# Padding the weight and activation tiles of a two-layer FFN by 32 bytes each

## The chip, the cores and the metric

The kernel runs on one core of one Trainium2 chip. The metric is the device time of one execution in microseconds (us), lower is better; a time of a kernel is the median over several runs, and the profile is of one execution.

## The reference

Talking-heads attention, then a gated feed-forward layer, then a second one; all in float32. B = 2, 12 heads, 448 positions, head size 64, so that 896 tokens of 768 features go through the two layers.

```
scores = (q @ k.T) / 8;  scores = mix(scores, w_pre)      # over heads
attn = softmax(scores);  attn = mix(attn, w_post)
x = (attn @ v) as [896, 768]
g = x @ w_gate;  u = silu(g) * (x @ w_val)                # d_ff 1536
x2 = u @ w_out
h = x2 @ w_in;   g = h * clip(h + 3, 0, 6) / 6            # d_ff 2048
out = g @ w_out2
```

## The kernel before

Attention comes first, some 205 us of the profiled span, and nothing in it is touched. Then five stages follow one another, named in the trace by the tiles that they fill: g and v in turn (12 output chunks each; PSUM tiles `pg`, `pv`), o (6 chunks, `po`), i (16 chunks, `pi`) and p (6 chunks, `pp`). A chunk is 128 output features for all 896 tokens, in two halves (`hf`) of 448 tokens.

Accuracy needs more than one product. Every operand is split into a high part (rounded to the type float32r) and a low part (the rest), and `product_half` makes three matmuls for each 128 input features: high weights by high activations, high weights by low activations, low weights by high activations, all 128x128 by 448 columns. There are 2448 of them: 36 for a g, v or i chunk, 72 for an o chunk, 96 for a p chunk.

The loop over `subs` (a sub is a chunk, or a part of one where the input has more than 768 features) keeps the weights ahead of the products. For sub j it issues, in this order: `halve(j+1)`, the split of the next weights (high part a copy on ACT, low part a subtraction on DVE, L402 and L404); `finish` of the sub before (PSUM to activations, on ACT and DVE); `convert(j+2)`, which makes float32 out of the 64-bit words that are loaded (ACT, then four DVE instructions, L462); the split of the activations just made (`rest()`: high part on ACT, L652; low part on POOL, L653); `fetch(j+3)`, the load of raw weights from SP's queue (L451); and the matmuls. All of DVE's work stands in one queue in this order.

The tiles are allocated from both ends of a partition's memory. From the left: `act`, the sixteen activation tiles a0 to a15, that hold u (12 of them) and later g (16), each 7168 bytes: high and low part by two halves of 448 float32r. From the right: raw and converted weights of the first two subs (`early`), four tiles `big` (x and x2, high and low, 10752 bytes each), the split weights of subs 0 and 1 (`wp0`), and `wp`: two raw tiles (`wr`), two converted (`wy`), three high and three low tiles of split weights (`wh`, `wl`, 3072 bytes each) and four scratch tiles (`sg`, 1792 bytes each).

In the program's allocation table this gives these start addresses in a partition, modulo 512: activation tiles all 160; x and x2 all 416; `wr`, `wy`, `wh`, `wl` all 96; `sg` 96 and 352 in turn. Inside a tile the slices are 1792 bytes (activations: 3.5 times 512) or 512 bytes (weights) apart. So, whatever tile a matmul uses, its activations start 64 bytes after its weights modulo 256 (64 or 320 modulo 512).

Of the kernel before, what the change touches and what calls it, by code (L numbers as in the profile page):

```python
# [8 lines left out]
F32R = mybir.dt.float32r  # L9
# [7 lines left out]
B, H, S, D = 2, 12, 448, 64  # L17
# [31 lines left out]
def kernel(  # L49
# [34 lines left out]
    pools = {"early": ctx.enter_context(tc.tile_pool(name="early", bufs=1, side="right"))}  # L84
# [311 lines left out]
        return y, todo  # L396

    def split_w(pool, y, kc, name):
        hi = pool.tile([128, kc, 128], F32R, name=f"h{name}", tag="wh", bufs=2 if pool is pools["wp0"] else 3)
        lo = pool.tile([128, kc, 128], F32R, name=f"l{name}", tag="wl", bufs=2 if pool is pools["wp0"] else 3)  # L400
        hi_flat, lo_flat = (x.rearrange("p k f -> p (k f)") for x in (hi, lo))
        nc.scalar.copy(hi_flat, y)  # L402
        eng = nc.gpsimd if pool is pools["wp0"] else nc.vector
        eng.tensor_tensor(lo_flat, y, hi_flat.bitcast(F32), ALU.subtract)  # L404
        return hi, lo
# [13 lines left out]
                pass  # L419

    def new_pair(nm, tg):
        t = act.tile([128, 2, 2, S], F32R, name=nm, tag=tg)
        return [(t[:, 0, hf, :], t[:, 1, hf, :]) for hf in range(2)]

    steps = []
# [38 lines left out]
    def halve(j):  # L464
        if j < len(subs):
            kind, idx, k0, kc, _ = subs[j]
            _, y, _ = ys.pop(j)
            pool = pools["wp0" if j < 2 else "wp"]
            whl[j] = split_w(pool, y, kc, f"{kind}{idx}_{k0}")
# [169 lines left out]
    act = ctx.enter_context(tc.tile_pool(name="act", bufs=1, side="left"))  # L639
# [7 lines left out]
    def finish(kind, idx, pp):  # L647
# [7 lines left out]
        if kind == "g":  # L655
            for hf in range(2):
                sg = scratch(f"sg{idx}_{hf}")
                nc.scalar.activation(sg, pp[hf][:, :S], AF.Sigmoid)
                nc.vector.tensor_tensor(sg, pp[hf][:, :S], sg, ALU.mult)
                sgs[hf] = sg  # L660
        elif kind == "v":
            us.append(new_pair(f"u{idx}", f"a{idx}"))
            for hf in range(2):
                sg = sgs[hf]
                nc.vector.tensor_tensor(sg, pp[hf][:, :S], sg, ALU.mult)
                late.append((us[-1][hf], sg, nc.gpsimd))
        elif kind == "o":
            for hf in range(2):
                if hf not in x2:
                    x2[hf] = [big.tile([128, HP, S], F32R, name=f"x2{part}{hf}", tag="big") for part in "hl"]  # L670
                parts(of_x2(idx, hf), pp[hf][:, :S], nc.vector)
        elif kind == "i":
            gs.append(new_pair(f"g{idx}", f"a{idx}"))
            for hf in range(2):
                sg = scratch(f"rl{idx}_{hf}")
                nc.scalar.activation(sg, pp[hf][:, :S], AF.Relu, bias=half, scale=1.0 / 6.0)
                nc.vector.scalar_tensor_tensor(sg, sg, 1.0, pp[hf][:, :S], ALU.min, ALU.mult)  # L677
                late.append((gs[-1][hf], sg, nc.gpsimd))
        else:
            for hf in range(2):  # L680
                o, sz = HALVES[hf]
                ob = scratch(f"ob{idx}_{hf}")
                nc.scalar.copy(ob, pp[hf][:, :S])
                nc.sync.dma_start(out=outT[idx * 128 : (idx + 1) * 128, o : o + sz], in_=ob)
# [104 lines left out]
```

## Time and profile before

| | us |
|---|---|
| median of three runs | 687.66 |
| the runs | 687.36, 687.66, 691.33 |
| the profiled execution's own time | 685.68 |
| its span, first to last instruction | 683.9 |

The profiled execution is 1.98 us under the median, and 1.78 us of it lie outside the span. Of the span PE is busy 98%, DVE 74%, ACT 43% and POOL 22%; the granted TensorE clock is 1.00 throughout. A busy time of PE includes the pipelined ends of matmuls, so that two matmuls in a row overlap in it: how fast they go is read from the distance of their starts.

### The profile page before, as it was taken

How to read it: one execution, taken by the hardware profiler on the slowest of the kernel's cores; microseconds unless marked ns; L12 is line 12 of the kernel's file. 1: busy time of each engine (PE TensorE's matmuls, PEld its weight loads, DVE VectorE, ACT ScalarE, POOL GpSimd, SP SyncE). 2: the span in 40 equal slices, each digit the busy share in tenths (PEclk: the TensorE clock that was granted, in tenths of full speed). 3: DMA queues.
4: the chain of work that ended last, by engine and by line, in shares of the span. 5: the costliest groups of instructions: out<-in, count | busy, mean ns of one | idle time of the engine just before them, and what ended most of it. 6: DMA issues, size and time to landing. Idle time of an engine off the chain costs nothing.

```text
span 683.9 us, 16079 instructions
## 1 busy us (share of the span) xinstructions
PE 667.5 (98%) x6685; PEld 566.0 (83%) x6685; DVE 505.5 (74%) x836; ACT 297.1 (43%) x603; POOL 147.2 (22%) x179
## 2 busy tenths in 40 slices
PE   9989999999899999999999999999999999999997
PEld 3456656566689999999999999999999999999997
DVE  4678789898548888888887566668888888665550
ACT  4557667676433434343433323234554453332320
POOL 2423435435301131113111000013334332000000
PEclk9999999999999999999999999999999999999999
DMA  6767774554212423342333323322332233454420
GB/s 223 216 203 204 209 204 137 170 154 139 94 46 96 135 96 118 113 138 95 110 121 116 115 93 107 124 93 93 108 123 93 92 92 118 150 157 145 150 66 27
DMA packets 34200, 86.86 MB, mean 127 GB/s; under 512 B 9328, under 2 KB 22016, under 8 KB 34128
## 3 DMA queue, kind: packets, MB, share of 16 engines
q1 hardware_dynamic: 26208, 81.14, 36.6%
q0 software_dynamic: 7200, 3.94, 2.5%
q8 instruction: 52, 0.85, 0.5%
q10 hardware_dynamic: 720, 0.76, 0.3%
q14 instruction: 20, 0.16, 0.1%
HBM read 62.37 MB, written 2.75 MB: 95 GB/s over the span
## 4 chain that ended last, share of the span: by engine, by line
PE 67%; DVE 21%; DMA 5%; ACT 4%; issue 1%; SPq 1%; ACTq 0%; DVEq 0%
PE pp L413 15%; PE po L413 13%; PE pv L413 12%; PE pg L413 12%; DVE yi L462 9%; DMA sx<-S 5%; PE pqk L170 3%; PE pav L293 3%; PE ppre L217 3%; PE ppost L263 3%; DVE rl L677 2%; PE p L413 2%; DVE yp L462 2%; DVE li L404 2%; ACT e L238 2%; DVE nm L230 2%
## 5 line engine op out<-in xcount | busy, mean ns | idle before, releaser
L413 PE MATMUL pp<-g,hp 128*128 128x448 f32 x384 | 107.5, 361 | 0.0
L413 PE MATMUL po<-u,ho 128*128 128x448 f32 x288 | 80.6, 361 | 0.0
L653 POOL TENSOR_TENSOR g<-rl,g 128x448 fp32r<-128x448 f32 x32 | 41.3, 1310 | 167.8 <-ACT g L652 167.8
L413 PEld LDWEIGHTS pp<-g,hp 128*128 128x128 f32 x384 | 71.9, 187 | 5.5
L238 ACT ACTIVATE e<-ppre,nm 128x448 f32<-128x448 f32 x90 | 56.2, 630 | 38.9 <-DVE nm L230 38.7
L206 POOL DMA_DIRECT2D sx<-S x90 | 52.0, 578 | 93.9 <-issue 21.2
L413 PE MATMUL pp<-g,lp 128*128 128x448 f32 x192 | 69.8, 364 | 0.2 <-DVE lp L404 0.2
L413 PE MATMUL pi<-x2h,li 128*128 128x448 f32 x192 | 69.7, 363 | 0.0
L413 PE MATMUL pi<-x2l,hi 128*128 128x448 f32 x192 | 69.6, 362 | 0.0
L413 PE MATMUL pi<-x2h,hi 128*128 128x448 f32 x192 | 69.1, 360 | 0.0
L653 POOL TENSOR_TENSOR u<-sg,u 128x448 fp32r<-128x448 f32 x24 | 32.6, 1379 | 151.7 <-ACT u L652 151.7
L263 PE MATMUL ppost<-wn,e 60*64 60x60 f32 x2520 | 53.5, 221 | 4.1 <-issue 3.4
L413 PEld LDWEIGHTS po<-u,ho 128*128 128x128 f32 x288 | 54.0, 187 | 3.9
L230 DVE TENSOR_REDUCE nm<-ppre 128x1 f32<-128x448 f32 x90 | 52.0, 616 | 4.9 <-PE ppre L217 3.0
L217 PE MATMUL ppre<-sx,W 64*64 64x448 f32 x360 | 52.4, 545 | 2.0 <-issue 1.2
L293 PEld LDWEIGHTS pav<-at,v 128*64 128x64 f32 x576 | 28.0, 136 | 31.7 <-ACT xs L336 15.3
L263 PEld LDWEIGHTS ppost<-wn,e 60*64 60x64 f32 x2520 | 46.4, 134 | 7.9 <-issue 3.8
L413 PE MATMUL po<-u,lo 128*128 128x448 f32 x144 | 52.3, 363 | 0.0
L170 PE MATMUL pqk<-k,q 64*64 64x448 f32 (+3 forms) x384 | 48.5, 547 | 1.0 <-issue 1.0
L413 PE MATMUL pg<-xh,lg 128*128 128x448 f32 x132 | 47.9, 363 | 0.0
L413 PE MATMUL pv<-xh,lv 128*128 128x448 f32 x132 | 47.9, 363 | 0.0
L413 PE MATMUL pg<-xl,hg 128*128 128x448 f32 x132 | 47.8, 362 | 0.0
(97 smaller groups left out, 1397.2 us busy)
## 6 DMA issues: line engine op xcount, KB each, us to landing
sx<-S SPq DMA_DIRECT2D x90, 182.0 KB
ri<-in_moe_w_in_dram SPq DMA_DIRECT2D x16, 768.0 KB
ro<-in_moe_w_out_dram SPq DMA_DIRECT2D x12, 768.0 KB
rg<-in_moe_w_gate_dram SPq DMA_DIRECT2D x11, 768.0 KB
rv<-in_moe_w_val_dram SPq DMA_DIRECT2D x11, 768.0 KB
rp<-in_moe_w_out_dram SPq DMA_DIRECT2D x12, 640.0 KB
rp<-in_moe_w_out_dram SPq DMA_DIRECT2D x6, 768.0 KB
sx<-S POOLq DMA_DIRECT2D x90, 42.0 KB, 5.7
```

The costliest lines, as they stand in the source:

```text
L170: nc.tensor.matmul(p[e][lo:hi, :S], lhsT=qs[t][r, base + lo : base + hi], rhs=ks[b][r, c, :], start=True, stop=True, tile_position=(64 * e ...
L206: nc.gpsimd.dma_start(out=sx[m // 2][104:128, m % 2, :], in_=rows)
L217: nc.tensor.matmul(p[a][64 * r : 64 * r + 64, :S], lhsT=W1[rows, :], rhs=x[rows, r, :], start=True, stop=True, tile_position=(64 * a, 64 * r),
L230: nc.vector.tensor_reduce(nm[:, a : a + 1], pre[i][a][:, :S], AX.X, ALU.max, negate=True)
L238: nc.scalar.activation(e2[a], p[a][:, :S], AF.Exp, bias=nm[:, a : a + 1], scale=1.0, accum_out=sm[:, a : a + 1])
L263: nc.tensor.matmul(p[s][64 * c : 64 * c + 64, at, :, :], lhsT=e2[a][rows, 64 * k : 64 * k + 64], rhs=wn[rows, a, :].rearrange("p (g k) -> ...
L293: nc.tensor.matmul(p[64 * e : 64 * e + 64, : 2 * n], lhsT=vs[b][:, jc, h, :], rhs=ats[t][:, 2 * jc : 2 * jc + 2, h, :n], start=jc == 0, st ...
L404: eng.tensor_tensor(lo_flat, y, hi_flat.bitcast(F32), ALU.subtract)
L413: nc.tensor.matmul(p[:, :S], lhsT=wt[:, kk, :], rhs=xx, start=start, stop=stop)
L462: f(*args)
L653: eng.tensor_tensor(to[1], src, to[0].bitcast(F32), ALU.subtract)
L677: nc.vector.scalar_tensor_tensor(sg, sg, 1.0, pp[hf][:, :S], ALU.min, ALU.mult)
```

## The change

The six tiles of split weights in `wp` become 776 float32r long instead of 768 (3104 bytes for 3072), and the sixteen activation tiles 1800 instead of 1792 (7200 bytes for 7168). The two pairs of tiles in `wp0` stay as they were. The pads are neither written nor read: each tile is cut to its old size at once and then shaped as before, so that every instruction has the operands and sizes that it had, and only the addresses differ. No instruction is added, removed or moved.

```
     def split_w(pool, y, kc, name):
-        hi = pool.tile([128, kc, 128], F32R, name=f"h{name}", tag="wh", bufs=2 if pool is pools["wp0"] else 3)
-        lo = pool.tile([128, kc, 128], F32R, name=f"l{name}", tag="wl", bufs=2 if pool is pools["wp0"] else 3)
-        hi_flat, lo_flat = (x.rearrange("p k f -> p (k f)") for x in (hi, lo))
+        own = pool is not pools["wp0"]
+        hi, lo = (
+            pool.tile([128, 768 + 8 * own], F32R, name=f"{part}{name}", tag=f"w{part}", bufs=2 + own)[:, : kc * 128]
+            for part in "hl"
+        )
+        hi_flat, lo_flat = hi, lo
+        hi, lo = (x.rearrange("p (k f) -> p k f", f=128) for x in (hi, lo))
...
     def new_pair(nm, tg):
-        t = act.tile([128, 2, 2, S], F32R, name=nm, tag=tg)
+        t = act.tile([128, 4 * S + 8], F32R, name=nm, tag=tg)[:, : 4 * S]
+        t = t.rearrange("p (part hf s) -> p part hf s", part=2, hf=2)
```

The starts after it, modulo 512, follow from the sizes. Activation tile i: 160 + 32 i, so that the sixteen take every multiple of 32 once. `wp` grows by 192 bytes towards the left, with its right end in place: `wr` and `wy` 416; the three `wh` 416, 448, 480; the three `wl` 0, 32, 64; `sg`, x, x2 and the tiles of `wp0` as before. Activations now start after their weights by many multiples of 32 modulo 256: for x and x2 by 0, 224, 192 (high weights) and 160, 128, 96 (low weights), for u and g by each of the eight.

## Rows read from the trace of the kernel before

**Rows 1.** The page: busy time by engine, and the chain that ended last.

```profile
PE 667.5 (98%) x6685; PEld 566.0 (83%) x6685; DVE 505.5 (74%) x836; ACT 297.1 (43%) x603; POOL 147.2 (22%) x179
...
PE 67%; DVE 21%; DMA 5%; ACT 4%; issue 1%; SPq 1%; ACTq 0%; DVEq 0%
```

**Rows 2.** Busy us and counts by stretch: PE, PEld, DVE, ACT, POOL; clock, DMA.

```profile
205.00:363.00 158.00, 158.00 (x792) 148.09 (x791) 133.38 (x162) 60.37 (x92) 29.99 (x22) 1.00 0.34 113
363.00:449.50 86.50, 86.50 (x434) 81.08 (x433) 56.47 (x72) 25.75 (x36) 2.60 (x2) 1.00 0.35 114
449.50:578.50 129.00, 128.83 (x645) 120.31 (x643) 110.16 (x119) 60.33 (x100) 41.29 (x32) 1.00 0.30 97
```

**Rows 3.** The chain that ended last, 150 us on: start, us, what.

```profile
204.71 7.20 PE pg L413 x36
...
363.11 86.40 PE po L413 x432
449.51 7.21 PE pi L413 x36
...
578.53 101.89 PE pp L413 x508
```

**Rows 4.** Line 413, one row per pair of operands: ns minimum/median/maximum.

```profile
L413 PE MATMUL pi<-x2h,hi x192: 360/360/360, 449.3 to 563.9; 128*128 128x448 f32 x192
...
L413 PE MATMUL pg<-xh,lg x132: 363/363/363, 204.9 to 355.5; 128*128 128x448 f32 x132
```

**Rows 5.** Line 495, the clock-keeping matmuls: durations in ns.

```profile
L495 PE MATMUL clock<-idle x13: 366/581/607, 1.2 to 15.2; 128*128 128x480 bf16 x13
```

**Rows 6.** Timeline of PE, first 40 us: start, duration, the second clock-keeping batch.

```profile
14.21 1.38 PE L495 MATMUL clock<-idle 128*128 128x480 bf16 x6
```

**Rows 7.** Timeline of weight loads, line 170: first and last of ten.

```profile
9.96 0.14 PEld L170 LDWEIGHTS pqk<-k,q 64*56 64x56 f32 x4 [0.24 <-issue]
...
13.35 0.14 PEld L170 LDWEIGHTS pqk<-k,q 64*56 64x56 f32 x4 [0.23 <-issue]
```

**Rows 8.** Groups by form, 380 to 445 us: busy us, mean ns, idle before.

```profile
L404 DVE TENSOR_TENSOR lo<-yo,ho 128x768 fp32r<-128x768 f32 x8 | 7.7, 958 | 7.4 <-ACT ho L402 7.4
...
L402 ACT CAST ho<-yo 128x768 fp32r<-128x768 f32 x8 | 6.7, 834 | 26.1 <-DVE yo L462 26.1
```

**Rows 9.** Groups by form, 582 to 660 us.

```profile
L404 DVE TENSOR_TENSOR lp<-yp,hp 128x640 fp32r<-128x640 f32 x9 | 7.4, 825 | 7.4 <-ACT hp L402 7.4
...
L402 ACT CAST hp<-yp 128x640 fp32r<-128x640 f32 x9 | 6.5, 727 | 26.4 <-DVE yp L462 26.4
...
L462 ACT ACTIVATE yp<-rp 128x768 f32<-128x768 f32 x4 | 3.6, 894 | 4.5 <-DMA rp<-in_moe_w_out_dram 4.5
```

**Rows 10.** Timeline of DVE, 496 to 505 us.

```profile
496.57 1.98 DVE L462 TENSOR_SCALAR yi<-yi 128x768 f32<-128x768 f32 x2
498.58 2.79 DVE L462 SCALAR_TENSOR_TENSOR yi<-ri,yi 128x768 uint32<-128x768 uint32 x2
502.27 0.96 DVE L404 TENSOR_TENSOR li<-yi,hi 128x768 fp32r<-128x768 f32 x1 [0.90 <-ACT hi L402]
...
504.21 1.98 DVE L462 TENSOR_SCALAR yi<-yi 128x768 f32<-128x768 f32 x2
```

**Rows 11.** Timeline of POOL, 496 to 505 us.

```profile
496.97 2.59 POOL L653 TENSOR_TENSOR g<-rl,g 128x448 fp32r<-128x448 f32 x2 [5.06 <-ACT g L652]
```

**Rows 12.** The chain that ended last, 496 to 504 us.

```profile
498.58 1.80 DVE yi L462
```

**Rows 13.** Line 653 on POOL: ns minimum/median/maximum.

```profile
L653 POOL TENSOR_TENSOR g<-rl,g x32: 1151/1305/1474, 458.8 to 573.9; 128x448 fp32r<-128x448 f32 x32
```

**Rows 14.** Timeline of PE, 576.5 to 580 us.

```profile
577.75 0.58 PE L413 MATMUL pp<-g,hp 128*128 128x448 f32 x2
578.53 0.47 PE L413 MATMUL pp<-g,lp 128*128 128x448 f32 x1 [0.20 <-DVE lp L404]
```

**Rows 15.** The chain that ended last, 556 to 582 us.

```profile
577.65 0.84 DVE lp L404
```

## The prediction

> **What bounds the kernel now.** I read the shares first [rows 1]: PE is busy 98% of the span and makes up 67% of the chain that ended last, DVE 21%. Then the stretches [rows 2], since a share over the whole span hides which stage has what limit: behind the attention PE is busy without a break, at the full clock, and DVE is next. Then the distance of the matmuls' starts, from the chain [rows 3]: a chunk of 36 takes 7.20 us, the 432 of stage o take 86.40, the 508 that end stage p 101.89. That is 200.0, 200.0 and 200.6 ns for one. So the FFN is 2376 matmuls (2448 less the 72 of subs 0 and 1) at 0.2 us, or 475.2 us, and next to nothing else. The reader is to see that this rate is flat: the same in a stage that reads x, one that reads u and one that reads g.
>
> Stage i is the exception that matters. There DVE's turn of one chunk comes back after 504.21 - 496.57 = 7.64 us [rows 10], more than the 7.20 that PE needs. DVE starts with a lead of buffers and loses 0.44 us of it with each of the 16 chunks. At the end of that, in the second sub of stage p, the lead is gone: the matmul that needs the low weights starts at 578.53 where 577.75 + 0.40 = 578.15 was due [rows 14], because `lp` was made until 578.5 [rows 15]. PE loses 0.38 us there. So PE sets the end, and at one point, 578 us, DVE stands right behind it with no margin.
>
> **The change, part by part.** It adds, removes and moves no instruction, and changes no wait by intent. What it can change is the time that an instruction takes at another address. I go through who touches the moved tiles.
>
> *Allocation and waits.* The activation tiles grow to 115200 bytes from address 1184 and end at 116384; the lowest tile of `wp` goes from 117344 to 117152. Both lie over tiles of the attention, as before, and these are last used before the FFN's activations are written. A wait for them would be long satisfied. Cost 0; the cover is the order of the stages itself.
>
> *PE, 2376 matmuls and as many weight loads.* Before, activations start 64 bytes after their weights modulo 256, always; after, by eight different distances. Does the distance matter? Within the kernel before, 64 and 320 modulo 512 both occur, and high, low and all three buffers of each, and the duration of one kind does not move by more than 1 ns over 132 or 192 instances [rows 4]. That tests modulo 512, not modulo 256. For modulo 256 the nearest rows are the scores in the attention: the keys lie at one place modulo 256, the slices of q move on by 480 bytes a chunk, that is by 32 less than a multiple of 512, and ten groups of four weight loads (five chunks) start (13.35 - 9.96) / 9 = 0.377 us apart without one that differs by more than 0.01 [rows 7]. So five distances, one rate, though for plain float32 matmuls of 64 by 64. I take 0 for PE, by this row. The bounds: the only row of a stream without such a double read of four-byte operands is the clock-keeping batch, bf16 with 480 columns, (1.38 - 0.366) / 5 = 0.203 us from start to start [rows 5, 6]. Scaled to 448 columns that is 189.1 ns, 10.9 below the 200.0. If the 10.9 is a collision of weight load and stream, it could go, or, at other distances, come a second time: -10.9 to +10.9 ns for each.
>
> The Trainium skill speaks to this twice, and against itself. "SBUF — State Buffer", section "Who interferes with whom", says that the ports of TensorE for the moving operand and for the weights are independent and that only the port pair shared by VectorE and GpSimd brings contention: by that the change is worth nothing on PE. "TensorE: Matmul & The Clock Gate", section "Back-to-back issue gap", gives N/2.4 + 2.5 ns at the full clock: 202.5 for 480 columns, where the row gives 203, but 189.2 for 448, where the row gives 200.0; by it 2376 times 10.8 ns, 25.7 us, are an excess that something causes.
>
> *ACT and DVE, the split of the weights.* This pair is the best test of the idea in the trace, since `wy`, `wh` and `wl` all start at 96 modulo 512: three operands in step on the same place. DVE's subtraction takes 958 ns for 768 elements and 825 for 640, ACT's copy 834 and 727 [rows 8, 9]; that is 1.04 and 0.84 ns an element, on top of the same 0.16 and 0.19 us at either size. With POOL idle (the 958 of stage o) and with POOL at work (0.96 in stage i [rows 10]) it is the same. Above, a gain has nowhere to go: outside stage i DVE waits for others anyway, and in it PE can use no more than its 0.38 us. Below, the nearest row of a stretch by other traffic is that spread, under 0.005 us, 0.1 us over 16 chunks. I take 0.
>
> *POOL, the low part of u and g.* Two instructions a chunk. They take 1151 to 1474 ns [rows 13], and here DVE hangs on it: POOL's pair of 496.97 to 499.56 [rows 11] lies over a DVE instruction that began at 498.58 and took 1.80 us [rows 12], where the next of the same form took 2.79 - 1.80 = 0.99 [rows 10]. It ended 0.82 us after POOL did. So a longer POOL instruction lengthens DVE's 7.64 one for one. Bounds: all at 1.15 shortens the chain by 2 x 0.16 x 16 = 5 us, of which PE can use the 0.38 that it lost; all at 1.47 adds 5.3 us, and as there is no margin at 578 us it all lands on the end. I take 0: the scratch tile moves neither modulo 256 nor 512, and the two halves, which start 256 apart, make no two kinds of rows.
>
> *DMA.* Raw weights land 192 bytes lower, 416 instead of 96 modulo 512. ACT waits for one in stage p for 4.5 us in all [rows 9], while PE goes on; cover enough. 0.
>
> The sum is 0: a profiled execution of 685.7, which stands 2.0 under the median of its runs, so 687.7 as a median.
>
> **The rivals.** *The excess on PE is a collision and the new distances end it.* For it: 10.9 ns that the bf16 rows don't have. Against it: the flat rates [rows 4, 7], and that it would have to end for all eight distances. Price: stage g and v 792 x 10.9 = 8.6 us (DVE has 158 - 133 = 25 us idle there [rows 2]), o 4.7, stage i nothing, as DVE's 7.64 is above 7.20 already, p 508 x 10.9 = 5.5; 18.9 in all, 668.7.
>
> *The present distance of 64 is a good one and the new ones are worse.* This is the slower end, by one mechanism, in PE's reading of two operands at once. For it: no row shows a 128 by 128 float32r matmul at another distance modulo 256. Against it: rows 7. It decides by how many distances collide. If only equal places do, it hits two of nine matmuls in g and v (176), one in eight in o and p (126); stage i hides its share, since 7.20 + 0.09 stays below 7.64. 302 x 10.9 = 3.3 us, 691. If all but 64 do: all 792, seven in eight of 1008, 1674 x 10.9 = 18.2 us, 706; the i chunks come to 7.59 and stay hidden.
>
> *POOL slows, DVE passes PE.* The 5.3 us from above, from 578 us back: 693.
>
> *The pads do not do what they say.* The tiles do come to different places, but any pair of operands that meets in one instruction may have had no quarrel to begin with. That is the forecast's own time, and its chance stands in the forecast's.
>
> **How the numbers follow.** No change 0.84; faster by PE 0.05; slower by PE at equal places 0.03, at all but one 0.05; slower by POOL 0.03. A difference of 1%, 6.9 us, is about what a measurement of this kernel tells from none. Faster by more than that: 0.05. Slower: the 706 alone, 0.05. Within: 0.84 + 0.03 + 0.03 = 0.90. The range goes from 684.5, just under the profiled execution, to 693.0, which takes in the POOL bound and equal places; 0.10 and the scatter of runs stay outside.
>
> **What would show it.** In the changed kernel the chunks of 36 should still take 7.20 us in each stage, `lo` 958 ns and `ho` 834, POOL 1.15 to 1.47 us, DVE's turn in stage i 7.64, and PE's one short loss should stand near 578 us. A rate that differs between buffers or between activation tiles, some chunks 7.20 and others 7.3 or more, would be the collision at single distances. A rate below 200 ns anywhere would make the forecast wrong at its root; a turn of DVE over 7.64 with 200 ns kept would point at POOL.

## The result and the profile after

The changed kernel takes 694.18 us in the median of 18 runs, the one before 687.51 in 18: the ratio is 1.0098, with a 95% interval of 1.0079 to 1.0117. One run of the changed kernel, of 699.33 us, counts as slow and is not in the ratio. It is slower by 6.7 us, outside the forecast range by 1.2 us and on its slow side. The profiled execution took 693.29 us, its span is 691.5, 7.6 more than before, at a granted clock of 1.00.

The page of the changed kernel, busy time and the chain that ended last:

```profile
PE 674.2 (97%) x6685; PEld 566.5 (82%) x6685; DVE 507.0 (73%) x836; ACT 297.2 (43%) x603; POOL 146.8 (21%) x179
...
PE 89%; DVE 5%; ACT 2%; DMA 2%; issue 2%; POOL 1%; SPq 0%; ACTq 0%; POOLq 0%
```

Against [rows 1], PE is busy 6.7 us longer with the same 6685 instructions, the others as long as they were to within 1.5 us. DVE is gone from the chain (21% to 5%): PE alone now sets the end of the FFN. The chain itself says where (start, us, what):

```profile
204.47 7.35 PE pg L417 x36
211.82 7.36 PE pv L417 x36
219.17 7.30 PE pg L417 x36
226.48 7.36 PE pv L417 x36
...
365.96 87.79 PE po L417 x432
453.75 117.45 PE pi L417 x576
571.19 116.85 PE pp L417 x576
```

In [rows 3] a chunk took 7.20 us. Now two of three take 7.36 and the third 7.30, over and over: a pattern of three, and there are three buffers of split weights. Stage o went from 86.40 to 87.79, 203.2 ns a matmul. Stages g and v (22 chunks) took 161.49 us for 158.40. Stage i takes 117.45 for 115.2, stage p 116.85 for 115.7 (up to 578.53 + 101.89), its short loss at 578 us included. That is +3.1, +1.4, +2.2 and +1.1, in all 7.9 us; the FFN begins 0.24 us earlier, and the rest is the 7.6 of the span.

The other engines did not move. Groups by form from 380 to 445 us, and line 658 on POOL (ns minimum/median/maximum):

```profile
L408 DVE TENSOR_TENSOR lo<-yo,ho 128x768 fp32r<-128x768 f32 x8 | 7.7, 958 | 7.4 <-ACT ho L406 7.4
L406 ACT CAST ho<-yo 128x768 fp32r<-128x768 f32 x8 | 6.7, 834 | 26.1 <-DVE yo L467 26.1
```

```profile
L658 POOL TENSOR_TENSOR g<-rl,g x32: 1149/1298/1481, 463.2 to 578.3; 128x448 fp32r<-128x448 f32 x32
```

These answer [rows 8] and [rows 13] to the nanosecond or nearly so. So the time came from how far apart TensorE's matmuls start in time, and from nothing else.

### The profile page after: what moved, and what is told of

Read it like the earlier page. It is cut to its first block, busy times and chain, and to the rows that moved or that the text cites. A ratio compares the mean times of both kernels' runs of the same rounds, so it can differ in the third digit from the quotient of the medians.

```text
span 691.5 us, 16079 instructions
## 1 busy us (share of the span) xinstructions
PE 674.2 (97%) x6685; PEld 566.5 (82%) x6685; DVE 507.0 (73%) x836; ACT 297.2 (43%) x603; POOL 146.8 (21%) x179
## 4 chain that ended last, share of the span: by engine, by line
PE 89%; DVE 5%; ACT 2%; DMA 2%; issue 2%; POOL 1%; SPq 0%; ACTq 0%; POOLq 0%
PE pi L417 17%; PE pp L417 17%; PE po L417 13%; PE pv L417 12%; PE pg L417 12%; PE pqk L170 4%; PE ppre L217 4%; PE pav L293 4%; PE ppost L263 4%; PE p L417 2%; PE pav L313 2%; ACT e L238 2%; DVE nm L230 1%; DMA sx<-S 1%; DVE wn L250 1%
## 5 line engine op out<-in xcount | busy, mean ns | idle before, releaser
L417 PE MATMUL pp<-g,hp 128*128 128x448 f32 x384 | 109.0, 365 | 0.0
L293 PEld LDWEIGHTS pav<-at,v 128*64 128x64 f32 x576 | 28.0, 136 | 32.4 <-ACT xs L336 16.7
L417 PE MATMUL pv<-xl,hv 128*128 128x448 f32 x132 | 48.3, 366 | 0.0
```

Of the source, the lines that this page charges most:

```text
L293: nc.tensor.matmul(p[64 * e : 64 * e + 64, : 2 * n], lhsT=vs[b][:, jc, h, :], rhs=ats[t][:, 2 * jc : 2 * jc + 2, h, :n], start=jc == 0, st ...
L417: nc.tensor.matmul(p[:, :S], lhsT=wt[:, kk, :], rhs=xx, start=start, stop=stop)
```

## The experiments

Theory A: a float32r matmul is held up by the load of weights that runs beside it, and by how much depends on where its activations start after the weights, modulo 256; call that the distance. It was 64 everywhere before. Theory B: ACT, DVE or POOL get in PE's way. In what follows "rate" is the settled time from start to start of a chunk's matmuls, worked out from the trace's starts: the median over stretches of nine, so that the first few after a change of distance do not count. The plain mean of a chunk is within 0.7 ns of it. A kernel named with "one run" was timed once; there the trace counts and not the time.

**One half of the change at a time.** Weight tiles padded only:

```
-        t = act.tile([128, 4 * S + 8], F32R, name=nm, tag=tg)[:, : 4 * S]
-        t = t.rearrange("p (part hf s) -> p part hf s", part=2, hf=2)
+        t = act.tile([128, 2, 2, S], F32R, name=nm, tag=tg)
```

> Only the six weight tiles padded; activation tiles as before. Theory A (distance): a float32r matmul takes the longer, the worse the start of its moving operand lies modulo 256 against the start of the weights that are loaded beside it; 200.0 ns at the old distance of 64. It expects stages g, v and i as in the changed kernel (chunks of 7.36, 7.36, 7.30 us in turn), o and p near 204 ns a matmul too, since the distances there are now the same six, in all 7 to 9 us slower than before. Theory B (the other engines: DVE, ACT and POOL write into tiles that PE reads, and the pads moved them into each other's way): the weight tiles are written by ACT and DVE, so slower too, but the rate should depend on how busy DVE and ACT are, with p's last part, where DVE is half idle, back at 200.

697.36 us against 687.08, ratio 1.0138 (1.0085 to 1.0191). The chain of this kernel:

```profile
204.34 7.35 PE pg L417 x36
211.68 7.36 PE pv L417 x36
219.04 7.30 PE pg L417 x36
...
365.82 88.08 PE po L417 x432
453.90 117.46 PE pi L417 x576
571.36 117.42 PE pp L417 x576
```

Each chunk goes by its weight buffer: 204.4, 204.4 or 202.9 ns, the same in all five stages, to the last part of p where DVE is half idle. By the trace this is 8.7 us more than before (484.4 against 475.7 from the first chunk on), within the 7 to 9 expected; the medians stand 10.3 apart. With the activations unpadded they are all at 160 modulo 256, and u and g stand where x stands; the stages become alike. B asked for the opposite.

Activation tiles padded only (the weights as before):

> Only the sixteen activation tiles padded; weights as before. Theory A: g, v and i back at exactly 200.0 ns (distance 64 again), o and p above it, with a rate that changes from activation tile to activation tile and repeats after eight tiles: some 3 us slower than before in all. Theory B: g, v and i stay slow where ACT and POOL write the padded activation tiles (they write u in g and v, g in i), o and p, where nobody writes them, at 200.

688.8 us, ratio 1.0008 (0.9982 to 1.0035): too little for these runs to tell from nothing, but the trace shows it in place. From its chain:

```profile
348.52 7.20 PE pg L413 x36
355.72 7.20 PE pv L413 x36
362.92 87.39 PE po L413 x432
...
579.38 103.24 PE pp L413 x508
```

g and v are at 200.0 again, while POOL and ACT write padded tiles all through them. o costs 1.0 us more than in [rows 3] and the end of p 1.35, together 2.3 of the 3 us expected. The finer forecast, a rate by activation tile that repeats after eight, does not hold: the three matmuls on a8, which stands at 64 as a0 does, go at 202.3 to 202.7 ns in the first half of each o chunk and at 199.7 to 200.0 in the second. What ran just before matters too. So the weights' pads carry the loss: they shift every one of the 2376 matmuls, the activations' pads only the 1008 of o and p. The two are no sum either: from the first chunk's start to the end of the chain's last the changed kernel takes 483.6 us, the weights' pads alone 484.4.

**A pad that keeps the distance.** The weight tiles 256 bytes longer, the spacer beside `big` 256 shorter:

```
+            pool.tile([128, 768 + 64 * own], F32R, name=f"{part}{name}", tag=f"w{part}", bufs=2 + own)[:, : kc * 128]
...
-    ctx.enter_context(tc.tile_pool(name="shift", bufs=1, side="right")).tile([128, 80], F32, name="shift1")
+    ctx.enter_context(tc.tile_pool(name="shift", bufs=1, side="right")).tile([128, 16], F32, name="shift1")
```

> The six weight tiles padded by 256 bytes in place of 32 and the spacer tile shortened by 256, so that all weights still start at 96 modulo 256 but at 96 and 352 modulo 512 in turn; activations as before. Theory A, with the distance modulo 256: 200.0 ns everywhere, the time of before (0.998 to 1.002). Theory A with modulo 512: some chunks slower. Theory C (a pad of any kind between the tiles costs): as slow as the changed kernel's weight part, 1.01.

685.57 us, ratio 0.9988 (0.9964 to 1.0012): no change. Every chunk is at 200.0, but for the two around 578 us, where DVE is late as it was before. From its chain:

```profile
204.46 7.20 PE pg L417 x36
...
362.86 86.40 PE po L417 x432
...
578.40 101.89 PE pp L417 x508
```

So neither a pad nor the place modulo 512 costs anything.

**All sixteen distances in one run.** Sub j slices its weights at another place of the longer tiles:

```
+        at = own * (4 * (j % 16))
+        hi_flat, lo_flat = (x[:, at : at + kc * 128] for x in (hi, lo))
```

> As the kernel with pads of 256 bytes, but sub j puts its high and low weights 16 * (j mod 16) bytes into their tiles, so that one run shows all sixteen distances 64 - 16 m modulo 256, each for a whole chunk. Theory A: each chunk has its own rate, the same for the same distance in every stage: 200.0 at 64, about 201.8 at 32, 204 at 0, 203 at 128 to 224 and the worst, about 207, at 96; those at odd multiples of 16 in between. Theory B: the rate goes by stage and by what DVE and ACT do, not by j mod 16.

694.72 us in one run. Rates in ns, one column per distance; the stages agreed to 0.4 except where two values stand (and a 202.2 in p at 112):

```
distance   0     16    32           48    64    80    96    112
rate     202.7 203.4 204.4/206.7  204.4 200.0 203.3 205.3 204.4
distance 128    144   160          176   192   208   224   240
rate     204.0 204.0 200.0        203.3 202.2 202.2 204.4 206.7
```

Three chunks from the chain, at distances 32, 160 and again 32:

```profile
205.84 7.36 PE pg L418 x36
...
264.48 7.20 PE pg L418 x36
...
323.02 7.43 PE pg L418 x36
```

In this run the rate goes by the distance and, but for 112 in p, not by stage or by what DVE does: it fits A and not B. But my table of values, taken from the changed kernel's trace, was poor (I had 207 for 96 and 203 for 160), and at 32 one and the same distance has two rates. Nothing is below 200.0.

**All matmuls at one distance.** The same kernel with a constant place, 80 bytes or 160:

```
+        at = own * (20)      # and 40
```

> All high and low weights 80 bytes into tiles that start at 96 modulo 256, so that every activation operand starts 240 bytes after its weights modulo 256; nothing else differs from the kernel with pads of 256 bytes. Theory A: every matmul of the 2376 at 206.67 ns, the rate that the scan showed at 240: 15.8 us more, of which 0.4 replaces the loss of before at 578 us, so 702 to 703, ratio 1.022, and DVE no longer late in stage i. Theory B (other engines in the way): the addresses that ACT and DVE write are moved alike for all tiles, so no more than the changed kernel's 1.010.

702.24 us, ratio 1.0242 (1.0213 to 1.0271). The chain shows one rate from end to end, 7.44 / 36 = 206.7:

```profile
202.92 7.44 PE pg L418 x36
...
366.60 89.28 PE po L418 x432
455.88 119.04 PE pi L418 x576
574.92 119.05 PE pp L418 x576
```

> The same with 160 bytes: the distance is 160 modulo 256 everywhere, another place than before for every weight tile. Theory A: the scan showed 200.00 there, so the time of before, ratio 0.997 to 1.003. Theory B, and the plain reading that only the old place was good: slower by 1%.

686.79 us, ratio 1.0019 (0.9993 to 1.0045), and 200.0 in all stages but for the short loss near 577 us, where DVE is late:

```profile
354.93 7.20 PE pv L418 x36
362.13 86.40 PE po L418 x432
577.40 101.89 PE pp L418 x508
```

Both moved every weight tile by the same kind of step; one costs 16.7 us, the other nothing that these runs tell. The old place is not the only good one.

**Only the low weights moved.** High weights stay at 64, low ones go through the sixteen places (`hi` from 0, `lo` from `at`).

> High weights stay at distance 64; only the low weights of sub j lie 16 * (j mod 16) bytes into their tile. Of three matmuls (high weights twice, low weights once) one loads low weights and one multiplies with them. Theory A, weights that are loaded beside a running matmul: the start that is delayed is that of the matmul with low weights (it waits for its load beside the second high one). Rival: the weights in use matter, and the start after the low one is delayed. In both the mean of a chunk rises by about a third of what the scan of both showed, up to 202.2 at 240 and nothing at 160.

690.73 us in one run. The question stays open: the delay is spread over the three starts, and the rates do not add. With low weights at 224 a chunk stays at 200.0, where both at 224 gave 204.4; at 0 it takes 204.4 in all chunks but one, where both gave 202.7. At 160, where nothing was expected, it takes 203.3, while both at 160 gave 200.0. The highest was 204.5, twice the expected rise.

**Steps of 4 bytes.** `at = own * (j % 64)`.

> Sub j puts its weights 4 * (j mod 64) bytes into the tiles: 64 distances in steps of 4 bytes. Theory A with the distance counted in lines of 16 bytes or coarser: the rates of the sixteen known distances, with steps between them. A finer dependence: values between or beyond, perhaps below 200.0, in which case there would be a faster place than the old one.

693.54 us in one run. The lowest of the 64 places is again 200.0 (at eleven of them: 4, 8, 16, 32, 56, 64, 116, 148, 160, 220 and 236), the highest 211.7, at 92. There are finer steps than 16 bytes, but no faster place in the one or two chunks that each place had. Also, 16 and 32 show 200.0 here, where the scan before had 203.4 and up to 206.7.

**PE alone.** Bursts of matmuls on x2 and g after the last product, all other engines idle:

```
+    for away in list(range(0, 256, 16)) + list(range(240, -1, -16)):
+        burst(48, 448, away)                 # float32r, 48 matmuls
+    for away in (64, 160):
+        for cols in (128, 192, 256, 320, 384, 448, 512):
+            burst(48, cols, away)
+    for away in range(0, 256, 16):
+        burst(24, 448, away, BF)             # the same bytes read as bf16
```

> The kernel before, followed by bursts of matmuls on x2 and g when everything else is done (their results are not used): 48 with 448 columns at each of the sixteen distances, upwards and then downwards, then 128 to 512 columns at distances 64 and 160, then bf16 at the sixteen distances. No other engine works by then. Theory A: the float32r bursts show 200.0 to 207 ns by distance, as in the scan, without any other engine. Theory B: 200.0 throughout. Of columns: if the floor of 200.0 is a fixed 13.3 ns on top of the columns, 384 columns take 173.3 and 512 take 226.7. Of bf16: it reads half the bytes, and if the collision is between two reads of four-byte operands its bursts stay at 189 to 190 at every distance.

With nothing else at work the rates are there: upwards 206.7, 202.2, 206.7, 203.0, 200.0, 203.3, 205.3, 206.7 for 0 to 112 and 204.2, 206.7, 200.0, 204.2, 202.2, 204.0, 203.4, 202.7 for 128 to 240. Downwards most repeat, but 0 gives 202.7, 32 gives 200.0, 160 gives 206.7 and 224 gives 204.4. From the timeline of PE (start, duration): the first and last matmul of the two bursts at 160 and of the upward one at 240; then the second of the first bf16 burst and the first of the next, 23 matmuls on.

```profile
777.27 0.37 PE L735 MATMUL bench<-x2h,g 128*128 128x448 f32 x1
...
786.68 0.36 PE L735 MATMUL bench<-x2l,g 128*128 128x448 f32 x1
...
825.94 0.37 PE L735 MATMUL bench<-x2h,g 128*128 128x448 f32 x1
...
835.47 0.36 PE L735 MATMUL bench<-x2l,g 128*128 128x448 f32 x1
...
884.53 0.37 PE L735 MATMUL bench<-x2h,g 128*128 128x448 f32 x1
...
894.24 0.37 PE L735 MATMUL bench<-x2l,g 128*128 128x448 f32 x1
...
1097.20 0.35 PE L735 MATMUL bench<-x2l,g 128*128 128x448 bf16 x1
...
1101.55 0.35 PE L735 MATMUL bench<-x2h,g 128*128 128x448 bf16 x1
```

At 160, 47 steps in 9.41 us and in 9.71: 200.2 and 206.6 ns for the same operands at the same places. At 240, 47 steps in 9.53 us: 202.8. 23 bf16 steps in 4.35 us: 189.1, and so at each of the sixteen distances (189.2; within a burst no step is off by more than 1 ns, but for the very first, 199, behind float32r). Columns at distance 64: 146.7 ns for 320, 173.3 for 384, 200.0 for 448; that is 0.417 ns a column and 13.3 ns on top. The expected 226.7 for 512 was missed (229.0, and 234.2 at distance 160), and 128 and 192 columns both take 111.6.

So the rate hangs on addresses with PE alone, and B falls for good. Neither place is bad by itself: weights at 160 modulo 256, where all of these bursts have them, go at 200.0 with activations at 224; activations at 160, as in the kernel before, go at 200.0 with weights at 96; both at 160, which is distance 0, took 202.7 in the scan and 206.7 and 202.7 here. It is the pair that counts. But "as in the scan", as A had it, is only half true. Nine of the sixteen distances show a rate that the scan showed too; 16, 48, 112, 144, 176, 208 and 240 do not, and 240, at 206.7 in every kernel above that has all weights of a chunk there, is at 202.7 in both of its bursts. The distance alone does not give the rate.

The bf16 bursts differ by more than the width of what is read: their weight loads are shorter too (mean 98 ns against 188), so that they lie beside half of a stream, the float32r ones beside nearly all of it.

```profile
L735 PEld LDWEIGHTS bench<-x2l,g 128*128 128x128 f32 x1078 | 202.8, 188 | 14.4
...
L735 PEld LDWEIGHTS <-g 128*128 128x128 bf16 x384 | 37.5, 98 | 35.2 <-issue 0.3
```

**What came before.** Even subs at distance 32, odd ones through all sixteen (`at = own * (8 if j % 2 == 0 else 4 * (j // 2 % 16))`).

> Even subs have their weights at distance 32, odd ones go through all sixteen. In the scans one and the same distance gave several rates (32: 200.0, 204.4 and 206.7). Theory D, what came before decides as well (the load of weights slips against the stream, and the slip that it enters with settles into one of several steady patterns): the even chunks show two or three different rates, by the distance of the chunk before them, not by their buffer. Theory E, the place of the buffer decides (modulo more than 256): the even chunks' rate goes with j modulo 3.

691.95 us in one run. Three chunks at distance 32, from the chain; before them ran chunks at 64, 48 and 16:

```profile
201.23 7.36 PE pg L418 x36
...
215.95 7.44 PE pg L418 x36
...
245.58 7.20 PE pg L418 x36
```

Even chunks ran at 200.0, 204.4 or 206.7, and outside stage p the rate followed the chunk before: behind 16, 240 and 192 it was 200.0 both times, behind 0, 224, 208 and 48 it was 206.7 both times, in different buffers each time. Behind 64 it was 204.4 once (sub 2) and 206.7 once, at another stage. In p, where parts of 30 matmuls stand between, 112, 128 and 96 gave other rates than earlier. Odd chunks at 160 ran at 206.7 here, 200.0 in the scan. So the distance alone does not fix the rate, and neither does the buffer (theory E falls): what ran before decides among a few steady patterns. Whether the last chunk or more than that, this run does not tell, since the sequence of distances repeats as a whole.

## Why the prediction was wrong

*PE at no cost.* This is the step that failed. I took 0 for PE "by this row", the scores [rows 7], as the nearest to a matmul at another distance modulo 256. They are plain float32 matmuls of 64 by 64; the float32r bursts show that the rows nearest in place were not nearest in kind. The row itself says how far off it is: a group takes 0.377 us, its weight loads 0.14 of that with 0.23 idle behind them, where in the FFN a load of 187 ns lies beside nearly all of the 200 of a stream:

```profile
L413 PEld LDWEIGHTS pp<-g,hp 128*128 128x128 f32 x384 | 71.9, 187 | 5.5
```

The term measured (571.19 + 116.85 - 204.47) / 2376 = 203.5 ns a matmul instead of 200.2 before, some 3.3 ns or 7.9 us. It lies well within the -10.9 to +10.9 of the bounds, which the range then did not use. I had written that [rows 4] test modulo 512 and not modulo 256; that was right, the pad of 256 bytes shows modulo 512 to be free, and it left the question that mattered without a row.

*The rival that came true* is the second: "the present distance of 64 is a good one and the new ones are worse". That the rate hangs on how the two operands of PE lie came true; that a collision in reading them is the reason is not shown. Neither price was right: equal places alone gave 691, all but 64, at 10.9 ns each, 706. The distances cost 0 to 6.7 at steps of 16 bytes, and the changed kernel 3.3 on average, a third of 10.9. The two versions had 0.08 between them, with no row against them but the wrong one.

*Stage i was to hide its share*, since 7.29 stays below DVE's 7.64. It did not: 117.45 us for 115.2. DVE's turn is still 7.64 us in the changed kernel (500.97 to 508.61), but it only eats into a lead, and in the kernel before that lead lasted until 578 us; the whole wait that PE could save from 449.5 us to there was the 0.38 at the end. The cover is what is left at the end of the lead, not the difference of two turns. That 0.38 was indeed recovered: the chain after has no DVE behind 205 us.

*The excess of 10.9 ns* would not go by any distance: no place of 64, in steps of 4 bytes, was below 200.0 in any run, and the first rival falls. The excess itself is real: 189.2 for bf16 in the bursts (the 189.1 scaled from [rows 5, 6] should have come to 189.3), 200.0 at best for float32r. The Trainium skill, "TensorE: Matmul & The Clock Gate", section "Back-to-back issue gap", gives N/2.4 + 2.5 ns at the full clock for an isolated matmul, an estimate of 189.2 for 448 columns. The bf16 bursts agree with it, although each of their matmuls has a weight load beside it; the float32r ones do not. The Trainium skill, "SBUF — State Buffer", section "Who interferes with whom", has the two read ports of TensorE independent. For bf16 the bursts agree; for float32r, with every other engine idle, a rate that hangs on where the two operands lie does not, and the measurement decides.

*ACT, DVE, POOL, DMA and waits at 0* held, point by point: 958, 834, 1149 to 1481 ns, no new wait. ACT's wait for raw weights in p was 4.4 us, 4.5 before. *The faster side* at 0.05 found none: no distance went below 200.0.

Open: which load meets which stream (moving the low weights alone did not tell), why a few patterns are steady at one distance, and why the bursts and the kernel differ at 240. That it is a collision of reads in the memory is argued from the dependence on both addresses and from the bf16 bursts, not shown; the shorter weight load of bf16 is a rival reason for its one rate, and no run parts the two.

## What to carry to other kernels

Where float32r matmuls with a weight load each are the bound, the start of the moving operand after the weights, modulo 256, is a tuning parameter: here worth up to 3% of their time (200.0 to 206.7 ns) in steps of 16 bytes. Hold it at a place that measures well, best at one that does so whatever runs before it, and re-measure when any tile on either side changes size. Pads that make addresses differ "for good measure" are no safe default. One distance for all is none either: at 64 and at 160 it was the best of these kernels, at 240 the worst. A pad of 256 bytes cost nothing. To bound an unseen cost, take the row of the same instruction in kind, or none, and then let the range have both ends.

## What was not expected of the hardware

At distance 64 every whole chunk and burst settled at 200.0, whatever came before; at 160, 32 and 0 the same burst settled at one of two rates (200.0 or 206.7; 200.0 or 206.7; 202.7 or 206.7). bf16 from the same places, half the bytes, knows no distance: 189.2 ns at all sixteen. A float32r matmul carries 13.3 ns on top of its columns from 320 to 448 columns, and with 192 it takes the same 111.6 ns as with 128.
